# Decode attention on one core: keeping the identity loaded in the PE array through the 24 score matmuls of a head

## Chip, cores and metric

The kernel runs on one core of a Trainium2 chip. The metric is device time in microseconds (us) of one execution. Engines are named as in the profile: PE is TensorE's matrix multiplication, PEld its weight loads, DVE is VectorE, ACT is ScalarE, POOL is GpSimd, SP is SyncE, which here issues the transfers.

## The reference

The program applies four layers of single-token attention, A, B, A, B, to a vector of 640 numbers. Each layer has 32 heads of width 192 and a cache of 8192 keys and values per head. The weights and caches of A are used twice, as are those of B.

```python
def _A_ref(x, k_cache, v_cache, wq, wo):          # _B_ref is the same function on B's data
    q = (x @ wq).reshape(B, 1, 32, 192).transpose(0, 2, 1, 3)
    scores = jnp.einsum("bhqd,bhkd->bhqk", q, k) * (192 ** -0.5)
    p = softmax(scores)
    o = jnp.einsum("bhqk,bhkd->bhqd", p, v)
    return o.transpose(0, 2, 1, 3).reshape(B, 1, 32 * 192) @ wo

x = A_x
x = x + _A_ref(layernorm(x), A_k_cache, A_v_cache, A_wq, A_wo)
x = x + _B_ref(layernorm(x), B_k_cache, B_v_cache, B_wq, B_wo)
# ... and both once more
```

All data are bf16. One head's keys are 8192 x 192 x 2 bytes = 3.1 MB, and so are its values. With 32 heads and four layers some 800 MB of keys and values have to be read, and each element is used once per layer.

## The kernel before

Keys and values come in through eight slots of 3072 KB. SP issues a transfer as soon as the last reader of the slot's former contents is done, so several transfers are under way at once (a K tile lands 23 to 36 us after its issue in the median, and its 3.1 MB take 7.3 us at 430 GB/s). For one head the work is:

1. `products`: DVE multiplies the K tile (64 keys x 192 elements in each of 128 partitions) by the query, in place, in four quarters of 48 elements.
2. PE adds up over the 192 elements. It does so with the identity matrix as the stationary operand: each of 24 matmuls streams 512 columns (64 keys x 8 elements) and accumulates them into one PSUM bank. What is left after 24 of them are eight partial sums for each key, which DVE adds up in `softmax`.
3. `softmax` on DVE, PE, ACT; then `values` on PE, with two columns of probabilities as the stationary operand, in four column groups.

```python
def products(h):
    # ... choose the slots; DV.wait(K tile landed, query ready)
    for c in range(4):                                   # QD = 48, R = 8
        d0 = c * QD
        e = DV.op(lambda v, d0=d0: v.tensor_tensor(
            k3[:, :, d0:d0 + QD], kin[:, :, d0:d0 + QD],
            q_sb[qi][:, d0:d0 + QD].unsqueeze(1).broadcast_to([P, J, QD]), ALU.mult))
        chunks.append(e)
    S = SP_[par]
    # ... PE waits until the PSUM bank S is free
    for c in range(4):
        PE.wait(chunks[c])
        for r in range(QD // R):                         # six matmuls a quarter
            d0 = c * QD + r * R
            fin = c == 3 and r == QD // R - 1
            e = PE.op(lambda t, d0=d0, fin=fin: t.matmul(
                S[:, :], lhsT=ident[:], rhs=k3[:, :, d0:d0 + R],
                start=(d0 == 0), stop=fin), signal=fin, bank=use[f"S{par}"])
    freed[nt] = ev_S[h] = e                              # the K slot is free for the next transfer

def values(h):
    # ...
    for m in range(J // 2):
        g, j = m % G, 2 * m
        OB[par][32 * g:32 * g + 2, 0:2 * DH] += p_sb[par][:, j:j + 2].T @ t[:, j * DH:(j + 2) * DH]   # a matmul, shortened here
    # freed[V slot] = its last matmul
```

Every `t.matmul` becomes two instructions for PE: a load of `lhsT` into the array, and the matmul itself (the profile counts 10,438 of each). So each of the 24 score matmuls loads the same identity again.

## Time and profile before

| | before |
|---|---|
| time, median of the first 3 runs | 2005.2 us (2005.04 to 2006.86) |
| bytes moved by DMA | 850.85 MB, mean 424 GB/s over the span |
| PE busy / weight loads busy | 1402.4 us (70%) / 616.8 us (31%) |
| DVE busy | 1047.3 us (52%) |
| mean granted PE clock | 0.831 |

The granted clock is the share of full speed that PE's clock was given, as the profile records it. The first lines are from the page of the kernel before. After the busy times stand rows of 40 slices of the span (tenths of busy time, the PE clock in tenths, GB/s), then the DMA queues with packets, megabytes and their share of 16 engines' time, then the chain of work that ended last.

```profile
PE 1402.4 (70%) x10438; PEld 616.8 (31%) x10438; DVE 1047.3 (52%) x1072; ACT 217.2 (11%) x657; POOL 4.6 (0%) x22
...
PEclk9788888788678788878778888888886888987887
DMA  9999999999999999999989999999999999999997
GB/s 404 431 430 430 429 430 426 430 431 429 425 431 429 431 429 430 426 431 430 429 361 431 430 430 430 431 426 429 429 430 426 430 428 428 431 430 431 430 430 325
DMA packets 44067, 850.85 MB, mean 424 GB/s; under 512 B 4800, under 2 KB 7360, under 8 KB 7872
...
q1 hardware_dynamic: 43824, 849.37, 99.2%
q8 instruction: 82, 1.34, 0.3%
...
DMA 67%; PE 19%; DVE 12%; ACT 1%; issue 1%; another core or an unknown queue 0%; POOL 0%; DVEq 0%; ACTq 0%
```

The rate stands at 429 to 431 GB/s in nearly every slice, whatever PE and DVE do. The table of stretches says where it does not. Its columns are the stretch, its length, busy time and count of each engine, the PE clock, the share of time in which the DMA engines were busy, and GB/s.

```profile
40.00:1010.00 970.00, 678.28 (x4871) 293.41 (x4869) 506.52 (x506) 104.10 (x317) 0.55 (x1) 0.82 1.00 429
1010.00:1060.00 50.00, 35.52 (x494) 21.70 (x495) 17.58 (x27) 4.44 (x15) 0.54 (x1) 0.69 0.88 361
1060.00:1970.00 910.00, 643.38 (x4659) 277.71 (x4658) 491.51 (x495) 102.75 (x311) 0.54 (x1) 0.85 1.00 429
1970.00:2005.00 35.00, 26.07 (x251) 14.62 (x249) 14.99 (x17) 2.88 (x10) 0.00 (x0) 0.74 0.66 280
```

DMA is busy all the time in the two long stretches. It loses some 6 us (0.12 x 50 us) at the border of the two middle layers and stands idle at the end, while the last head is computed.

Next, the groups of the score work: line, engine, operation, names, shapes and count, then busy time, mean ns of one, idle time before them and what ended it.

```profile
L425 DVE TENSOR_TENSOR slot<-slot,q_sb 128x3072 bf16<-128x3072 bf16 x512 | 865.9, 1754 | 461.2 <-DMA slot<-in_A_k_cache_dram 236.2
L437 PE MATMUL S<-slot,ident 128*128 128x512 bf16 x3072 | 839.5, 429 | 286.6 <-DVE slot L425 286.6
L437 PEld LDWEIGHTS S<-slot,ident 128*128 128x128 bf16 x3072 | 307.8, 108 | 813.2 <-DVE slot L425 428.3
```

3,072 weight loads of the identity have 307.8 us of busy time, but that is on PEld, which overlaps PE: the median load starts 214 ns before its own matmul, while the matmul ahead runs. Whether they cost PE anything is seen in the spacing of the matmuls. The order of time on PE, near the end of the span (start, length, line, operation, count, and the idle time before):

```profile
1972.15 5.35 PE L437 MATMUL S<-slot,ident 128*128 128x512 bf16 x24
1977.87 1.47 PE L437 MATMUL S<-slot,ident 128*128 128x512 bf16 x6 [0.37 <-DVE slot L425]
1979.54 1.47 PE L437 MATMUL S<-slot,ident 128*128 128x512 bf16 x6 [0.20 <-DVE slot L425]
```

The 24 matmuls of 1972.15 take 5.35 us. The last has a record of 0.379 us, so 23 spacings fill 4.97 us: 0.216 us each. 512 columns in 0.216 us is one column in 0.42 ns. Shorter matmuls of this trace keep the same pace, though each has a load of its own: at full clock one of 128 columns is followed after 55 to 56 ns and one of 64 columns after 28 to 29 ns (line 377, whose loads have records of 98 ns). A load of 0.1 us between two matmuls would show there; so none seems to be left between the long ones either. The other two bursts shown come in sixes, because PE waits for DVE's next quarter (1.67 us against 1.47 us).

### The profile page before, as it was taken

The page shows a single profiled execution, that of the slowest core. Times are in us where ns is not written, and L with a number is a line of the kernel's source. Part 1 is how long each engine was busy: PE and PEld are TensorE (multiplying, and loading weights), DVE is VectorE, ACT ScalarE, POOL GpSimd, SP SyncE. Part 2 cuts the span into 40 slices and gives each one's busy share as a digit, 9 for nine tenths or more (in the row PEclk, how much of TensorE's full clock was granted, in tenths as well). Part 3 has the DMA queues.
Part 4 walks back from the last instruction along what each step waited for, and adds up shares of the span by engine and source line. Part 5 has one row for each costly group of instructions (what it writes and reads, how often), then busy time and mean ns, then how long its engine had stood idle before and what let it go on. Part 6 is the DMA issues. An engine that isn't in the chain of part 4 may idle for free.

```text
span 2005.0 us, 23356 instructions
## 1 busy us (share of the span) xinstructions
PE 1402.4 (70%) x10438; PEld 616.8 (31%) x10438; DVE 1047.3 (52%) x1072; ACT 217.2 (11%) x657; POOL 4.6 (0%) x22
## 2 busy tenths in 40 slices
PE   5677767767666767667777676676777767767667
PEld 2223223223332322322342232232234323323223
DVE  3454554556345456455536545545654455654554
ACT  0011011011011111111100111111110111111110
POOL 0000000000000000000000000000000000000000
PEclk9788888788678788878778888888886888987887
DMA  9999999999999999999989999999999999999997
GB/s 404 431 430 430 429 430 426 430 431 429 425 431 429 431 429 430 426 431 430 429 361 431 430 430 430 431 426 429 429 430 426 430 428 428 431 430 431 430 430 325
DMA packets 44067, 850.85 MB, mean 424 GB/s; under 512 B 4800, under 2 KB 7360, under 8 KB 7872
## 3 DMA queue, kind: packets, MB, share of 16 engines
q1 hardware_dynamic: 43824, 849.37, 99.2%
q8 instruction: 82, 1.34, 0.3%
q14 instruction: 17, 0.14, 0.0%
q10 hardware_dynamic: 144, 0.00, 0.0%
HBM read 849.35 MB, written 0.00 MB: 424 GB/s over the span
## 4 chain that ended last, share of the span: by engine, by line
DMA 67%; PE 19%; DVE 12%; ACT 1%; issue 1%; another core or an unknown queue 0%; POOL 0%; DVEq 0%; ACTq 0%
DMA slot<-in_A_k_cache_dram 33%; DMA slot<-in_B_k_cache_dram 32%; PE S L437 13%; DVE slot L425 10%; PE O L473 2%; DMA slot<-in_A_wq_dram 1%; PE TB L488 1%; DVE s_sb L444 1%; DMA x_bf<-in_A_x_dram 1%; ACT p_sb L454 1%; PE QT L358 1%; PE YB L394 1%; PE TB L458 0%; DVE small L451 0%
## 5 line engine op out<-in xcount | busy, mean ns | idle before, releaser
L425 DVE TENSOR_TENSOR slot<-slot,q_sb 128x3072 bf16<-128x3072 bf16 x512 | 865.9, 1754 | 461.2 <-DMA slot<-in_A_k_cache_dram 236.2
L437 PE MATMUL S<-slot,ident 128*128 128x512 bf16 x3072 | 839.5, 429 | 286.6 <-DVE slot L425 286.6
L437 PEld LDWEIGHTS S<-slot,ident 128*128 128x128 bf16 x3072 | 307.8, 108 | 813.2 <-DVE slot L425 428.3
L473 PE MATMUL O<-slot,p_sb 128*2 128x384 bf16 x4096 | 347.0, 420 | 0.0
L444 DVE TENSOR_REDUCE s_sb<-S 128x64 f32<-128x512 f32 x128 | 88.4, 691 | 248.6 <-PE S L437 248.6
L473 PEld LDWEIGHTS O<-slot,p_sb 128*2 128x2 bf16 x4096 | 128.5, 88 | 133.4 <-issue 97.6
L488 PE MATMUL TB<-o_sb,small 128*1 128x192 f32 x480 | 121.5, 385 | 36.6 <-DVE small L462 28.2
L384 ACT ACTIVATE q_sb<-QM 128x192 bf16<-128x192 f32 x120 | 39.6, 330 | 982.4 <-PE QM L377 982.4
L458 PE MATMUL TB<-small,ones 128*128 128x1 f32 x256 | 50.1, 265 | 110.0 <-ACT p_sb L454 110.0
L448 PE MATMUL QM<-ident,m_bf 128*128 128x128 bf16 x128 | 27.8, 217 | 129.6 <-DVE m_bf L447 129.6
L481 ACT ACTIVATE o_sb<-O,small 128x384 f32<-128x384 f32 x128 | 74.3, 580 | 231.0 <-PE O L473 231.0
L462 DVE RECIPROCAL small<-TB 128x1 f32<-128x1 f32 x128 | 21.6, 169 | 122.7 <-PE TB L458 122.7
L458 PEld LDWEIGHTS TB<-small,ones 128*128 128x128 f32 x256 | 39.3, 193 | 129.7 <-ACT p_sb L454 129.7
L454 ACT ACTIVATE p_sb<-s_sb,small 128x64 bf16<-128x64 f32 x128 | 44.5, 348 | 290.1 <-DVE small L451 290.1
L451 DVE TENSOR_REDUCE small<-QM 128x1 f32<-128x128 f32 x128 | 37.3, 292 | 53.7 <-PE QM L448 53.7
L494 ACT ACTIVATE orow<-TB 1x192 bf16<-1x192 f32 x120 | 38.3, 319 | 202.6 <-PE TB L488 202.6
L488 PEld LDWEIGHTS TB<-o_sb,small 128*1 128x1 f32 x480 | 33.2, 88 | 78.4 <-DVE small L462 37.4
L448 PEld LDWEIGHTS QM<-ident,m_bf 128*128 128x128 bf16 x128 | 12.3, 96 | 146.5 <-ACT q_sb L384 131.6
L394 PE MATMUL YB<-oT,slot 128*128 128x1 bf16 x900 | 37.9, 178 | 3.4 <-ACT oT L409 2.2
L394 PEld LDWEIGHTS YB<-oT,slot 128*128 128x128 bf16 x900 | 36.9, 131 | 4.2 <-ACT oT L409 2.9
L377 PEld LDWEIGHTS QM<-ident,qT 128*128 128x128 bf16 x240 | 23.0, 99 | 30.5 <-issue 1.9
L377 PE MATMUL QM<-ident,qT 128*128 128x128 bf16 x240 | 30.4, 209 | 1.6 <-ACT qT L366 1.6
(46 smaller groups left out, 191.0 us busy)
## 6 DMA issues: line engine op xcount, KB each, us to landing
slot<-in_B_k_cache_dram SPq DMA_DIRECT2D x64, 3072.0 KB, 36.1
slot<-in_A_k_cache_dram SPq DMA_DIRECT2D x63, 3072.0 KB, 23.4
slot<-in_A_v_cache_dram SPq DMA_DIRECT2D x63, 3072.0 KB, 25.9
slot<-in_B_v_cache_dram SPq DMA_DIRECT2D x60, 3072.0 KB, 37.5
slot<-in_A_wo_dram SPq DMA_DIRECT2D x6, 2400.0 KB, 26.7
slot<-in_B_wo_dram SPq DMA_DIRECT2D x6, 2400.0 KB, 34.9
slot<-in_A_wq_dram SPq DMA_DIRECT2D x4, 2880.0 KB, 22.5
slot<-in_B_wq_dram SPq DMA_DIRECT2D x4, 2880.0 KB, 29.7
```

The source lines that it names most:

```text
L377: e = PE.op(lambda t, b=b, o=o, n=n, d=done: t.matmul(QM[:, d:d + n], lhsT=qT[:, b:b + 1].broadcast_to([P, P]), rhs=ident[:, o:o + n], sta ...
L384: lambda a: a.activation(q_sb[i][:], QM[:, 0:DH], ACT.Copy), e, last["q"][i], bank=use["QM"])
L394: e = PE.op(lambda t, i=i, c=c, f=y_first[0], fin=fin: t.matmul(YB[:, c:c + 1], lhsT=t3[:, i, c:D:DC], rhs=o[:, i:i + 1], start=f, stop=fi ...
L425: e = DV.op(lambda v, d0=d0: v.tensor_tensor(k3[:, :, d0:d0 + QD], kin[:, :, d0:d0 + QD], q_sb[qi][:, d0:d0 + QD].unsqueeze(1).broadcast_t ...
L437: e = PE.op(lambda t, d0=d0, fin=fin: t.matmul(S[:, :], lhsT=ident[:], rhs=k3[:, :, d0:d0 + R], start=(d0 == 0), stop=fin), signal=fin, ba ...
L444: ev_s = DV.op(lambda v: v.tensor_reduce(s_sb[par][:], S[:].rearrange("p (j r) -> p j r", r=R), AX.X, ALU.add), ev_S[h], last["s"][par], b ...
L448: e = PE.op(lambda t: t.matmul(QM[:, C_MX:C_MX + P], lhsT=m_bf[par][:, 0:1].broadcast_to([P, P]), rhs=ident[:], start=True, stop=True), ev ...
L454: ev_p[h] = AC.op(lambda a: a.activation(p_sb[par][:], s_sb[par][:], ACT.Exp, bias=negm[par][:, 0:1], accum_out=l_col[par][:]), ev_n, ev_s ...
L458: e = PE.op(lambda t: t.matmul(TB[:, C_L + par:C_L + par + 1], lhsT=ones[:], rhs=l_col[par][:], start=True, stop=True), ev_p[h], last["L"] ...
L473: e = PE.op(lambda e, g=g, j=j, f=m < G, fin=fin: e.matmul(OB[par][32 * g:32 * g + 2, 0:2 * DH], lhsT=p_sb[par][:, j:j + 2], rhs=t[:, j * ...
L481: lambda a: a.activation(o_sb[:], OB[par][:, 0:2 * DH], ACT.Copy, scale=rl[par][:, 0:1]),
L488: e = PE.op(lambda t, i=i: t.matmul(TB[0:1, C_O:C_O + DH], lhsT=pick[:, i:i + 1], rhs=o_sb[:, i * DH:(i + 1) * DH], start=(i == 0), stop=( ...
```

## The change

The first matmul of a head loads the identity as before. The other 23 are issued as a bare matmul that uses the weights already in the array. The program gives PE no other matmul or load between them, so the weights should still be the identity. The intent is one weight load in place of 24.

```diff
+def matmul_held(t, out, lhsT, rhs, start, stop):
+
+    return t.add_instruction(mybir.InstMatmult(
+        name=t.bass.get_next_instruction_name(), engine=mybir.EngineType.PE,
+        ins=[t.lower_ap(rhs), t.lower_ap(lhsT, for_matmul_weights=True)], outs=[t.lower_ap(out)],
+        start_tensor_calc=start, stop_tensor_calc=stop, tile_size=(128, 128), tile_position=(0, 0), ldweights=False))
...
-                        e = PE.op(lambda t, d0=d0, fin=fin: t.matmul(S[:, :], lhsT=ident[:], rhs=k3[:, :, d0:d0 + R],
-                                                                     start=(d0 == 0), stop=fin), signal=fin, bank=use[f"S{par}"])
+                        e = PE.op(lambda t, d0=d0, fin=fin: (
+                            t.matmul(S[:, :], lhsT=ident[:], rhs=k3[:, :, d0:d0 + R], start=True, stop=fin) if d0 == 0 else
+                            matmul_held(t, S[:, :], ident[:], k3[:, :, d0:d0 + R], False, fin)), signal=fin, bank=use[f"S{par}"])
```

## The prediction

> **What bounds the kernel now.** DMA. The page's DMA line gives 850.85 MB at a mean of 424 GB/s; its row of slices shows 429 to 431 GB/s almost throughout. The table of stretches has DMA share 1.00 from 20 to 1010 us and from 1060 to 1980 us. The losses are the first 20 us (370 GB/s), the border between the two middle layers (1020 to 1060 us: 312, 323, 379 GB/s, some 6 us) and the tail after the last K tile (29 us from 1976 us). PE is busy 70%, DVE 52%. The chain of waits: DMA 67%, PE 19%, DVE 12%. PE's share there is mostly the matmul that freed a slot, while other transfers keep the queue full (a K tile lands 23 to 36 us after its issue; two tiles take 14.6 us at 430 GB/s).
>
> **What the change removes.** 23 of 24 identity loads a head: 2,944 of 3,072. In the groups all 3,072 cost 307.8 us, but on the load side. In the order of time, a burst of six score matmuls takes 1.47 us, the last 379 ns of it: spacing (1.47-0.38)/5 = 0.218 us. A burst of 24 in 5.35 us gives 0.216. [...] the loads are hidden already. At half clock loads show 0.15 us + 0.28 us idle, period 0.43 us, again the time of 512 columns at half rate. So spacings stay 0.216 and 0.427 us and PE busy stays near 1402 us (within 2%). Besides, most bursts are paced by VectorE's products (1.67 us a quarter against 1.47 us of matmuls). At the tail only the first load of the last burst could show: at most 0.1 us.
>
> **What it adds.** No operation. A small gain: the queue "instruction" moves 1.34 MB, as much as PE's 20,876 instructions at 64 bytes [...]. 2,944 fewer are 0.19 MB: an estimated 0.4 us at 429 GB/s; by that queue's share of time (0.3% of the span, 6 us) 14% of it is 0.85 us. DMA being the bound, this counts: -0.4 to -0.9 us.
>
> **Second order.** The clock toggles between 1.0 and 0.5 (mean 0.831). [...] at half clock a head's score matmuls take 10.2 us and its values 2.8 us of a 14.6 us period[...]. [...] tail (clock 0.50 in the last 15 us) and border may move 1 to 2 us either way, as the three runs of before do (2005.04 to 2006.86).
>
> **Predicted:** 2004.7 us, 8 in 10 within 2002.0 to 2008.0. Faster by over 2%: 0.01; within 2%: 0.97; slower: 0.02.
>
> **What would show it.**
> - Weight loads 10,438 -> 7,494, busy 617 -> about 320 us; spacing unchanged. If spacing falls, I was wrong on hiding.
> - DMA share stays 1.00 at 429 to 431 GB/s; instruction queue falls to about 1.15 MB, 70 packets.
> - Mean clock 0.80 to 0.86. [...]
> - VectorE's wait for score matmuls (248.6 us) stays.
>
> **What would make it wrong.** A matmul without its own load that issues with a bubble (bursts beyond VectorE's 1.67 us); a clock that stays at half; a chip with another DMA rate. Weights not kept across the waits between quarters would give a wrong result, not another time.

Marked cuts take out a formula for the spacing, a source, and conditions that took the clock to follow the loads, which no run here shows. The sum: 2005.2 us, the median of the first three runs, less 0.4 to 0.9 us, put at 2004.7 us. The 64 bytes are 1.34 MB over 20,876 instructions.

## The result, and the profile after

The changed kernel gives the right result. Ratios in this document are of one kernel's fast runs to the other's of the same rounds; they are not quite the ratios of the medians.

| | before | after |
|---|---|---|
| time, median of 4 runs each | 2006.03 us (2005.04 to 2007.02) | 2004.40 us (2002.56 to 2004.88) |
| ratio, 95% interval | | 0.9990 (0.9973 to 1.0008) |
| span of the profiled run | 2005.0 us | 2002.9 us |
| weight loads | 10,438, 616.8 us | 7,494, 323.9 us |
| instruction queue | 82 packets, 1.34 MB | 70 packets, 1.15 MB |

All these runs are fast (none is over 1.5% above the fastest of its kernel). The same lines of the page, after:

```profile
PE 1406.5 (70%) x10438; PEld 323.9 (16%) x7494; DVE 1047.1 (52%) x1072; ACT 217.6 (11%) x657; POOL 4.6 (0%) x22
...
PEclk8788888888688798787878888888886888887887
DMA  9999999999999999999999999999999999999997
GB/s 404 433 430 426 431 430 426 431 431 428 425 431 429 431 429 430 426 432 428 429 375 432 430 429 431 431 427 430 429 429 428 430 428 431 431 429 429 429 431 321
DMA packets 44055, 850.65 MB, mean 425 GB/s; under 512 B 4800, under 2 KB 7360, under 8 KB 7872
...
q1 hardware_dynamic: 43824, 849.37, 99.3%
q8 instruction: 70, 1.15, 0.2%
...
DMA 70%; PE 17%; DVE 12%; ACT 1%; issue 1%; another core or an unknown queue 0%; SPq 0%; DVEq 0%
```

PEld has lost half of its busy time; PE has lost none (1402.4 before, 1406.5 after). The rows of clock and rate look the same. On the instruction queue 12 packets are gone. The stretches of the changed kernel:

```profile
40.00:1010.00 970.00, 678.74 (x4872) 148.84 (x3431) 507.05 (x508) 104.42 (x317) 0.55 (x1) 0.83 1.00 429
1010.00:1060.00 50.00, 37.65 (x500) 16.68 (x454) 17.67 (x27) 4.66 (x14) 0.54 (x1) 0.69 0.92 375
1060.00:1970.00 910.00, 648.26 (x4676) 143.62 (x3288) 494.29 (x497) 103.12 (x312) 0.54 (x1) 0.84 1.00 430
1970.00:2003.00 33.00, 23.20 (x225) 9.29 (x185) 11.64 (x15) 2.38 (x8) 0.00 (x0) 0.71 0.61 261
```

The two long stretches have the same DMA share and rate within 1 GB/s. The border moves 375 GB/s where it moved 361; more of this below. The groups:

```profile
L58 PE MATMUL S<-slot,ident 128*128 128x512 bf16 x2944 | 795.6, 424 | 34.1 <-DVE slot L433 34.1
L446 PE MATMUL S<-slot,ident 128*128 128x512 bf16 x128 | 60.9, 476 | 249.4 <-DVE slot L433 249.2
...
L446 PEld LDWEIGHTS S<-slot,ident 128*128 128x128 bf16 x128 | 12.7, 99 | 331.3 <-DVE slot L433 330.9
```

128 loads are left, 12.7 us. The two matmul groups together, 795.6 + 60.9 = 856.5 us, are no shorter than the 839.5 us of before. The order of time on PE at the same place:

```profile
1975.74 0.39 PE L446 MATMUL S<-slot,ident 128*128 128x512 bf16 x1 [1.48 <-DVE slot L433]
1975.97 1.24 PE L58 MATMUL S<-slot,ident 128*128 128x512 bf16 x5
1977.40 1.46 PE L58 MATMUL S<-slot,ident 128*128 128x512 bf16 x6 [0.20 <-DVE slot L433]
1979.08 1.46 PE L58 MATMUL S<-slot,ident 128*128 128x512 bf16 x6 [0.21 <-DVE slot L433]
```

The burst still takes 1.46 to 1.47 us for six and still waits 0.2 us for DVE's next quarter. Over the whole trace, the commonest distance between the starts of two score matmuls is 216 ns in both kernels, with a second peak at 426 to 427 ns where the clock is at half.

The profiled runs differ by 2.1 us. None of it lies in the tail: from DVE's start on the last K tile to the end it is 28.95 us before (1976.05 to 2005.0) and 28.97 us after (1973.93 to 2002.9). Adding up the packets' times of each queue in the trace and dividing by 16 engines gives an account of the whole span:

| us of 16 DMA engines | before | before, second profile | after | after, second profile | after, third |
|---|---|---|---|---|---|
| data packets | 1988.96 | 1989.05 | 1988.53 | 1988.26 | 1988.08 |
| instruction packets | 5.46 | 5.48 | 4.67 | 4.66 | 4.67 |
| other | 0.58 | 0.59 | 0.58 | 0.60 | 0.57 |
| idle | 9.99 | 9.37 | 9.08 | 9.62 | 9.25 |
| span | 2004.99 | 2004.48 | 2002.86 | 2003.15 | 2002.58 |

The second profile of before is that of `idle_fetch` (experiment 5), whose edit left no mark on the chip. "Idle" is the span less the packets' times; it is a balance, because packets of one engine overlap a little (the DMA share reads 1.01 in some stretches).

The instruction packets give 0.8 us, and that repeats. Data packets are 0.4 to 1.0 us less. The idle rows overlap (9.4 and 10.0 before, 9.1 to 9.6 after). The profiled execution of before took 2007.09 us, more than any of its four timed runs, so 2.1 us probably overstates the gain.

The totals hide one difference that does repeat. In the slice with the border of the two middle layers (the 21st of the row GB/s) the unchanged kernel moved 361 and 364 GB/s, the changed one 375, 371 and 378. At 430 GB/s and 50 us a slice that is, by estimate, 0.8 to 2.0 us less lost there. In the last slice the changed kernel loses an estimated 0.5 to 0.8 us more (321 against 325 and 328). No experiment says whether the change does this, or how: phases of the clock (0.63 before and 0.74 after, from 1020 to 1025 us) and PE's wait for the query weights to land (2.08 and 0.82 us) differ there too.

### The profile page after: what moved, and what is told of

It is laid out like the page before. It is cut to its first block, busy times and chain, and to the rows that moved or that the text cites. A ratio compares the mean times of both kernels' runs of the same rounds, so it can differ in the third digit from the quotient of the medians.

```text
span 2002.9 us, 20412 instructions
## 1 busy us (share of the span) xinstructions
PE 1406.5 (70%) x10438; PEld 323.9 (16%) x7494; DVE 1047.1 (52%) x1072; ACT 217.6 (11%) x657; POOL 4.6 (0%) x22
## 3 DMA queue, kind: packets, MB, share of 16 engines
q8 instruction: 70, 1.15, 0.2%
## 4 chain that ended last, share of the span: by engine, by line
DMA 70%; PE 17%; DVE 12%; ACT 1%; issue 1%; another core or an unknown queue 0%; SPq 0%; DVEq 0%
DMA slot<-in_A_k_cache_dram 35%; DMA slot<-in_B_k_cache_dram 34%; PE S L58 11%; DVE slot L433 10%; PE O L482 2%; DMA slot<-in_A_wq_dram 1%; PE S L446 1%; PE TB L497 1%; DVE s_sb L453 1%; ACT p_sb L463 1%; PE TB L467 0%; PE QT L366 0%; DVE small L460 0%; PE YB L402 0%
## 5 line engine op out<-in xcount | busy, mean ns | idle before, releaser
L58 PE MATMUL S<-slot,ident 128*128 128x512 bf16 x2944 | 795.6, 424 | 34.1 <-DVE slot L433 34.1
L482 PE MATMUL O<-slot,p_sb 128*2 128x384 bf16 x4096 | 356.8, 428 | 0.0
L446 PE MATMUL S<-slot,ident 128*128 128x512 bf16 x128 | 60.9, 476 | 249.4 <-DVE slot L433 249.2
L453 DVE TENSOR_REDUCE s_sb<-S 128x64 f32<-128x512 f32 x128 | 88.4, 691 | 241.6 <-PE S L58 241.6
L446 PEld LDWEIGHTS S<-slot,ident 128*128 128x128 bf16 x128 | 12.7, 99 | 331.3 <-DVE slot L433 330.9
```

The source lines that it names most:

```text
L58: return t.add_instruction(mybir.InstMatmult(name=t.bass.get_next_instruction_name(), engine=mybir.EngineType.PE, ins=[t.lower_ap(rhs), t. ...
L446: t.matmul(S[:, :], lhsT=ident[:], rhs=k3[:, :, d0:d0 + R], start=True, stop=fin) if d0 == 0 else
L453: ev_s = DV.op(lambda v: v.tensor_reduce(s_sb[par][:], S[:].rearrange("p (j r) -> p j r", r=R), AX.X, ALU.add), ev_S[h], last["s"][par], b ...
L482: e = PE.op(lambda e, g=g, j=j, f=m < G, fin=fin: e.matmul(OB[par][32 * g:32 * g + 2, 0:2 * DH], lhsT=p_sb[par][:, j:j + 2], rhs=t[:, j * ...
```

## The experiments

The theory (A): DMA is the bound, the loads were hidden behind the matmuls anyway, and what is left is a little less instruction fetch. The rivals: (B) PE's loads did cost something, but DMA hides the gain, so it would show if DMA were not the bound; (C) the loads are hidden only because a 512-column matmul is long; (D) the small difference comes from PE freeing slots sooner, or is none.

### 1. The changed kernel again, twice

No edit. The second set ran on one chip with nine runs of before, the third on another chip with nine more.

> The changed kernel once more, to see whether its 0.1% is real. Theory A (the loads were hidden and DMA is the bound; only the instruction fetch shrinks by 0.19 MB, 12 packets of 16 KB): 0.4 to 0.8 us less than before, ratio 0.9996 to 0.9998, inside the noise. Rival B (PE frees slots earlier, so the border between the middle layers loses less DMA): 1.5 us or more less, ratio 0.9992 or below, with less DMA lost between 1020 and 1060 us. Rival C: no difference at all, ratio 1.0000. In all: 70 packets on the instruction queue, 7,494 weight loads, clock 0.82 to 0.84.

Measured: 2004.45 us against 2005.23, ratio 0.9995 (0.9982 to 1.0009), 70 packets, 7,494 loads, clock 0.832.

> The changed kernel a third time, for a smaller interval. The cut kernels cost 0.18 us for each packet of instructions that they add (13.1 us for 72, 4.2 us for 24). By that measure the change's 12 packets less are worth 2.1 us: ratio 0.9989. By my prediction's estimate, 0.4 to 0.9 us: ratio 0.9996 to 0.9998.

Measured: 2004.89 us against 2004.66 in the medians, ratio of the means 0.9996 (0.9984 to 1.0009).

What follows: the three ratios are 0.9990, 0.9995 and 0.9996, all below 1 and none outside noise. The means differ by 2.0, 0.8 and 0.7 us; in the third set the medians stand the other way round. Each interval is 2.5 us or more to either side, so these sets can't tell the 0.4 to 0.9 us of the prediction from the 2.1 us that I had by then read from experiment 5, nor from nothing. A gain of this size is suggested, not shown.

### 2. Make PE the bound: each score matmul four times

`quad_loads` is the kernel before, `quad_held` the changed one, with every score matmul repeated four times. The query is scaled by a quarter, so the result stays right.

```diff
-vs = -DH * nv + DH * EPS
+vs = -16 * DH * nv + 16 * DH * EPS        # rs = vs ** -0.5 becomes a quarter
...
-                        e = PE.op(... score matmul ...)
+                        for again in range(4):
+                            e = PE.op(... the same score matmul, start only the first time ...)
```

> The kernel before with each score matmul done four times (q at a quarter, so the result is the same), to make TensorE the bound. 96 matmuls of 512 columns a head at 0.216 us are 20.7 us; with the 5.4 us that lie between the last score matmul of a head and the first of the next, 26 us a head against 14.6 us of DMA: about 3340 us. DMA share near 0.58. If each load were paid for in full (98 ns), 96 x 0.098 = 9.4 us a head more: about 4550 us.

> The same with the identity held: one load a head in place of 96. If loads are hidden behind 512 columns: within 1% of the four-fold kernel with loads (about 3340 us), spacing 0.216 us. If the loads cost TensorE anything, this one is faster than it by up to 1200 us.

Measured: 3666.85 us with loads, 3664.26 us held; ratios to before 1.8279 and 1.8271. The groups of the first, then of the second, from their pages:

```profile
L438 PE MATMUL S<-slot,ident 128*128 128x512 bf16 x12288 | 2715.4, 383 | 24.5 <-DVE slot L425 24.5
```

```profile
L58 PE MATMUL S<-slot,ident 128*128 128x512 bf16 x12160 | 2679.5, 382 | 0.0
```

DMA is far from the bound here (its queue is busy 57.5% of the span, and DVE waits 7.5 us in all for the keys of A, against 236.2 us before), PE is busy 91%, 12,160 loads are taken away, and the time moves by 0.07%, within noise (had each load cost its record of 0.1 us, it would have been some 1200 us). The spacing is 216 ns in both. So B falls: at 512 columns the loads cost PE nothing that can be measured, though DMA is not the bound here. My 3340 us was too low for both alike: I took 26.1 us a head, and the median distance from a head's first score matmul to the next head's is 27.4 us; the rest I have not divided further. It does not bear on the comparison.

### 3. Shorten the matmul: 128 columns

Each score matmul is cut in four of 128 columns, and done twice so that PE stays the bound. The query is halved.

```diff
-                        e = PE.op(lambda t: t.matmul(S[:, :], lhsT=ident[:], rhs=k3[:, :, d0:d0 + R], ...))
+                        for again in range(2):
+                            for w in range(4):
+                                e = PE.op(lambda t: t.matmul(S[:, 128 * w:128 * w + 128], lhsT=ident[:],
+                                                             rhs=k3[:, 16 * w:16 * w + 16, d0:d0 + R], ...))
```

In `narrow_held` all but the first of a head are bare matmuls.

> The kernel before with each score matmul cut in four of 128 columns, and done twice (q at half), result the same: 192 matmuls with 192 loads a head. If the load still hides: spacing 0.056 us, 10.7 us of matmuls, some 16 us a head, 2060 to 2150 us. [...] If the load's 98 ns are the pace: 18.8 us, 24 us a head, about 3100 us.

> The same narrow matmuls with the identity held. Spacing 0.056 us at full clock: 16 us a head, 2060 to 2150 us, whatever the narrow kernel with loads takes. Faster than it by 20% or more if loads are exposed at 128 columns; equal if they are hidden there too. If a matmul without its own load had a bubble of its own, the spacing would stand above 0.056 us.

(0.056 us is the distance after a 128-column matmul on line 377 of the kernel before, at full clock.)

Measured: 2364.5 us with loads, 2362.24 us held; ratios to before 1.1786 (1.1767 to 1.1806) and 1.1765 (1.1723 to 1.1807). The commonest spacing is 56 ns in both. The order of time on PE of the kernel with loads: a whole head, 192 pairs, without a pause.

```profile
1015.65 10.89 PE L440 MATMUL S<-slot,ident 128*128 128x128 bf16 x192
```

(10.89 - 0.2) / 191 = 0.056 us a pair. A load whose record is 0.1 us long is hidden behind a matmul of 0.056 us. So the record's length is not the pace of loads: records of 0.1 us that start every 0.056 us overlap one another, too. C falls at this size. Both times are above my 2060 to 2150 us: the median distance from head to head is 17.45 us with loads and 17.26 us held, and only 10.9 us of it is the score burst.

### 4. Shorten it further: 32 columns

Sixteen matmuls of 32 columns in place of one, done once; otherwise as above (`w` in `range(16)`, slices of 32 columns and 4 keys).

> The kernel before with each score matmul cut in sixteen of 32 columns: 384 pairs a head. The trace of before has 90 pairs of a full load and a one-column matmul (the q projection) in 2.48 us: 27.6 ns a pair. If that is what a load takes as a pace, the spacing here is about 28 ns, 10.6 us a head, and the time near the narrow kernels' 2360 us. If each load is paid for in full after the matmul (13 + 28 ns), 41 ns, 15.7 us a head, near 3000 us.

> The same with the identity held. If the matmul's own stream of 32 columns (13.3 ns at full clock) sets the pace: 5.1 us a head, DMA is the bound again, about 2010 us. If a floor of some 25 ns for each matmul sets it [...]: 9.6 us a head, 5% below the sliver kernel with loads. Equal to it if loads are hidden even here.

(Both figures of the matmul can be had from the trace of before. 13.3 ns is an estimate from the distances after 128 and 512 columns, 32 x (216 - 56) / 384; some 25 ns is how far apart its pairs of a load and a one-column matmul start at full clock, line 358.)

Measured: 2837.59 us with loads, 2241.7 us held: 21% less (ratios to before 1.414 and 1.1173). Here the loads do cost time. But the commonest spacing does not say so: it is 25 to 27 ns held (the floor of some 25 ns that was expected) and 25 to 27 ns with loads. Even here a load and a matmul take no longer than a matmul alone, though the records of the loads are 100 ns long in the mean. The difference is elsewhere, as the group shows, in the column of idle time:

```profile
L440 PE MATMUL S<-slot,ident 128*128 128x32 bf16 x49152 | 1334.8, 182 | 519.7 <-issue 500.1
```

```profile
L58 PE MATMUL S<-slot,ident 128*128 128x32 bf16 x49024 | 1257.6, 178 | 0.3 <-issue 0.3
```

500.1 us of idle time before the matmuls with loads, ended by "issue", that is by nothing that another engine did; 0.3 us without loads. In the order of time on PE, with loads and then held:

```profile
1005.90 6.18 PE L440 MATMUL S<-slot,ident 128*128 128x32 bf16 x233
1016.02 3.56 PE L440 MATMUL S<-slot,ident 128*128 128x32 bf16 x128 [3.94 <-issue]
1019.77 0.74 PE L440 MATMUL S<-slot,ident 128*128 128x32 bf16 x23 [0.18 <-issue]
```

```profile
1002.22 9.86 PE L58 MATMUL S<-slot,ident 128*128 128x32 bf16 x383
```

PE runs 233 pairs, stands still for 3.94 us, runs exactly 128 pairs, and waits again. 128 pairs are 256 instructions. That is one packet of the instruction queue: its packets have 16,384 bytes in this trace, and `cut_loads_again` (experiment 5) has 72 of them more than before for 18,432 more instructions, 256 to a packet and 64 bytes to an instruction. I looked at all pauses of over 0.5 us within a burst: 237 of them, in 125 of 128 heads, 4.2 us a head together. All 112 that follow another pause in the same head come exactly 128 pairs after it. 90% of them end 1.23 to 1.57 us after the end of an instruction packet; for 90% of all instants that distance runs from 0.3 to 8.7 us. So the pauses end a steady time after a packet of instructions, as they would if PE waited for them. The held kernel has none (0.3 us in all). At 26 ns a pair, PE eats a packet's worth in 3.3 us, and the median interval between packets is 6.2 us, on engines that also carry the 3 MB tiles. Whether the tiles delay the packets was not tested.

What follows: at 32 columns the loads have a price (2837.59 us against 2241.7), and it goes with the length of the instruction stream (500.1 us of pauses against 0.3), not with time in the array (25 to 27 ns in both).

### 5. Fetch more instructions while DMA is the bound

First try: 5,000 no-operations on POOL in each layer.

```diff
             ev_rs = PO.op(lambda g: g.tensor_tensor(rs[:], vs[:], neghalf[:], ALU.pow), e, ev_const, last["qT"])
+            for _ in range(5000):
+                PO.op(lambda g: g.nop(), signal=False)
```

> The kernel before with 20,000 no-operations on GpSimd (5,000 after its one small operation of each layer), which touch no data: 1.28 MB more instructions, some 78 packets of 16 KB. Theory A, in the form that instruction fetch takes DMA time one for one: by the packets' time in the trace of before (82 packets took 87.4 us of one engine, 1.07 us each) 78 x 1.07 / 16 = 5.2 us more, so about 2011 us, ratio 1.0026; by bytes at 429 GB/s 3.0 us more, ratio 1.0015. Rival (fetches slip into gaps): below 1 us, ratio under 1.0005. PE, DVE and the clock as before.

Measured: 2006.51 us, ratio 1.0006 (0.9993 to 1.0019). This tells nothing of fetches: its trace has 82 packets on the instruction queue, the same packets in total and the same 23,356 instructions as before. As far as the trace shows, the no-operations never reached the chip. The run is in effect before against before, and shows what a ratio of nothing looks like: it lies about as far from 1 as those of the changed kernel.

Second try: the 128-column matmuls of experiment 3, done once. PE's work is nearly that of before (4 x 0.056 us against 0.216 us) and DMA stays the bound, but the instruction stream grows: by 72 packets with loads, by 24 held.

> The kernel before with each score matmul cut in four of 128 columns, done once: 96 pairs a head, 4 x 0.056 = 0.224 us in place of 0.216, so TensorE's work hardly changes and DMA stays the bound, but there are 18,432 more instructions: 1.18 MB, 72 packets on the instruction queue. If instruction fetch takes DMA time one for one: 72 x 1.07 / 16 = 4.8 us more by its packets' time, ratio 1.0024; by its bytes 2.7 us, ratio 1.0014. If fetches slip into gaps: ratio below 1.0005. If loads cost TensorE time that matters, more than either.

> The same with the identity held: 95 of 96 loads a head gone, 12,160 instructions, 0.78 MB, 47 packets fewer than the cut kernel with loads. Fetch one for one: 3.1 us (by bytes 1.8 us) less than it, and 1.6 us (0.9 us) more than before, ratio 1.0008. Fetch free and loads hidden: the same as before and as the cut kernel with loads.

Measured: `cut_loads` 2019.71 us, ratio 1.0065 (1.0051 to 1.0079); `cut_held` 2010.55 us, ratio 1.0021 (1.0007 to 1.0035). One run of `cut_loads`, the profiled one, took 4070.76 us: 128-column matmuls stood 210 ns apart, nearly four times the 56 ns, in every head, save the first three or so spacings of a head (402 in all are under 60 ns). The trace holds no record of the clock at all, so the 1.0 printed for it means nothing, and the cause is not known. It is left out, and the kernel was run again for a trace.

> The cut kernel with loads once more, because its profiled run fell in a state of its own (4068.7 us[...]) and four others took 2019.3 to 2020.2. Expected: about 2019.5 us again, and in a trace of a normal run: spacing 0.056 us or 0.106 us as in the cut kernel with the identity held; 154 packets on the instruction queue. If the extra 13 us are DMA's: data and instruction packets together take about 2006 us of 16 engines' time. If they are TensorE's: the packets take about 1999 us and the idle time of DMA grows by 9 us, with gaps in the score bursts.

Measured: 2019.38 us, ratio 1.0071 (1.0056 to 1.0086). Spacing 56 and 106 ns, as in `cut_held`. DVE's wait for score matmuls is 255.4 us, against 254.0 us in `cut_held`, and no spacing within a quarter's burst is over 107 ns (the half-clock spacing, a quarter of 427) in either: in the bursts PE is no later for its loads. The instruction queue on its page:

```profile
q8 instruction: 154, 2.52, 0.5%
```

| us of 16 DMA engines | before | cut_held | cut_loads_again |
|---|---|---|---|
| data packets | 1988.96 | 1989.37 | 1990.88 |
| instruction packets | 5.46 (82) | 7.08 (106) | 10.24 (154) |
| idle | 9.99 | 11.15 | 14.93 |
| other | 0.58 | 0.59 | 0.60 |
| span | 2004.99 | 2008.18 | 2016.65 |

The instruction packets' own time grows by 4.78 us for 72 packets, as expected (4.8). The span grows by more: 11.7 us in these profiles, 13 to 14 us by the ratios, some 0.18 us a packet, in the held kernel too (4.2 us for 24). The cleaner pair is `cut_loads` against `cut_held`, which have the same matmuls and ran in the same rounds: 9 us by the means for 48 packets and their loads, again some 0.19 us a packet. The rest of the growth over before is longer data packets (1.9 us) and more idle time (4.9 us). Packets of both kinds take 2001 us, which lies between the 2006 us expected if the extra were all DMA's and the 1999 us if it were PE's. Why idle time grows is open: it lies partly at the layer border (DMA share 0.87 from 1000 to 1060 us, against 0.90 before), partly in the tail, and I made no experiment on it.

What follows: in this kernel, which DMA bounds, more loads cost time though the spacing stays, and the packets' own time is a part of it that is seen. That the rest comes from fetch too is argued, not shown. 12 packets less are worth 0.8 us at the packets' own time, and 2.1 us at the 0.18 us of these kernels. The measured differences of the changed kernel, 0.7 to 2.0 us, lie about in that span. Of D, the unchanged spacing says that PE frees no slot sooner within a burst; at the layer border, where the changed kernel lost less, D is not excluded.

No experiment points to a version that beats both kernels: the bytes of keys and values set the time, and at 512 columns the loads had next to nothing to give.

## Why the prediction was right

- **The bound.** DMA: the long stretches stand at 1.00 share and 429 to 430 GB/s in both kernels. Right.
- **The loads are hidden.** The spacing stayed at 216 and 426 ns and PE busy at 1406.5 us (I had said within 2% of 1402). Experiment 2 shows that this is so when PE is the bound as well (216 ns with and without loads, 0.07% in the time), so it is not the DMA bound that hides a gain. The trace of before has it too, in its distances of 28, 56 and 216 ns for 64, 128 and 512 columns; the 307.8 us of busy loads were the trap.
- **What remains is instruction fetch.** I said 1.15 MB and 70 packets: measured 1.15 MB and 70. I said 0.4 to 0.9 us: the packets' time fell by 0.8 us, which is no more than 12 packets of 1.07 us on 16 engines. In the time itself the means differ by 0.7 to 2.0 us, within noise each time. Experiment 5 shows that more loads make a kernel of this kind slower; what 12 packets are worth in the time, and whether the border adds to it, is not shown.
- **The clock.** I said 0.80 to 0.86, and left open that it would change with the loads. The mean is 0.831 before and after, and 0.927 and 0.928 in the quadruple kernels, with 12,160 loads less: it did not.
- **The tail.** At most 0.1 us, I said; measured 28.95 and 28.97 us.
- **DVE's wait for score matmuls** went from 248.6 to 241.6 us. The second profile of before has 242.6 us, so this is the spread from run to run.
- **The time.** 2004.7 us predicted, 2004.4 us measured. That they agree to 0.3 us is partly luck: the changed kernel's own runs spread over 2.3 us, and before's median rose from 2005.2 us, from which I predicted, to 2006.03.

Where I was wrong was in the expectations of the experiments: I held it possible that a load shows at 128 columns (up to 98 ns a pair; these runs measured 56), and I expected the loads of the 32-column kernel to cost some 5%, in the array. Taking them away gave 21%, and not in the array: the spacing stayed at 25 to 27 ns, and 500.1 us of pauses went.

## What to carry to other kernels

Judge a weight load by the spacing of the matmuls around it, not by its busy time: where the matmuls stood 216 ns apart at 512 columns and 56 ns at 128, taking loads away left these distances as they were, even with PE as the bound. The busy share of the loads fell from 31% to 16% here, and from 42% to 9% in the quadruple kernels, with no change in time clear of noise. Count what the removed instructions weigh as bytes: in this kernel, which DMA bounds, it was the only return that could be traced to the change (12 packets, 0.8 us of their own time), and it is small. Holding the weights paid clearly only where matmuls were so short that PE stood still for instructions, as far as the pauses tell (here at 32 columns, 2837.59 us against 2241.7, with pauses exactly 256 instructions apart).
